# Three raw weight chunks move from SyncE's queue to GpSimd's, each behind a small copy

## The chip, the cores and the metric

One core of a Trainium2 chip runs the whole program. The metric is the device time of one execution in microseconds; the median of three runs counts. The engines are TensorE (PE; its weight loads are PEld), VectorE (DVE), ScalarE (ACT), GpSimd (POOL) and SyncE (SP). SP only issues DMA transfers.

## The reference, cut to what matters

```python
# q, k, v: (4, 8, 576, 64), s: (4, 8, 576)
scores = (1 / sqrt(64)) * q @ k.T
cum = cumsum(maximum(s, 0))
scores = where(causal, -1e9, scores + minimum(-(cum[:, None] - cum[None, :]), 0))
attn = softmax(scores) ; x = attn @ v            # heads side by side: (2304, 512)
h = x @ w_in                                     # moe:  512 -> 2048
x = (h * clip(h + 3, 0, 6) / 6) @ w_out          #       2048 -> 512
h = x @ w2_in                                    # moe2: 512 -> 2048
out = (h * (1 / (1 + exp(-h)))) @ w2_out         #       2048 -> 512
```

The weights are 64-bit numbers; everything else is 32 bits wide.

## The kernel before, in words

**Heads.** Each of the four batches is cut into a part A (256 query rows) and a part B (the other 320). With eight heads this gives 64 heads-with-a-part, here just called heads and numbered from 0 in the order in which they run; A of batch 0 comes first. Head n's tiles have a name, the part, the head's place among eight and a tile number: `pb1A_4_301` is a tile of head 4. A head goes through these steps: SP loads its q, k and v into one tile `in` and then a 4 KB piece of running sums (`inA<-pairs`, from head 4 on `inA<-pair_d`); TensorE makes scores (`ps0`, `ps1`); VectorE masks them and takes the row minimum (L540, `pb0`, `pb1`); ScalarE takes exponentials and their row sums (L558, into one of four tiles `sums`); VectorE adds a small number and takes the reciprocal of the sums (L566, L567); TensorE transposes (`pt`); ScalarE copies the result (`th`); TensorE multiplies by v (`po`); VectorE scales (`xt`). Two such heads are transposed to one piece (`px`, `xA`), which ScalarE and VectorE split into a high and a low half (`xh`, `xl`).

**Slots.** The program is written as slots. In slot k, head k makes its scores, head k-1 (`p1`) its transposes and its product with v. In the first nine slots heads run alone. In that time TensorE also gets three dummy products per head (`keep_clock`, tile `idle`), which read the head's `pb1` tile. From slot 9 on each slot also has a step of the first layer pair: products with `w_in` (`ph`), a gate (`g`, `gh`, `gl`), products with `w_out` (`acc`).

**Weights.** Both layers are cut into 16 chunks each of `w_in` and `w_out`, 512 KB as they lie in memory. They are named i0, o0, i1, o1, ... here (tiles `rawi_0`, `rawo_0`, ...). SP loads a raw chunk (L147); ScalarE makes two passes over it (`fields`, L159 and L160); GpSimd one (L162); VectorE joins the results (L178, L182); ScalarE rounds them to a high half (L120) and VectorE takes the low half (L193). The class `Feed` does this in ticks: at a tick one chunk is asked for, and the one asked for three ticks earlier begins its passes. Three ticks come ahead of slot 0 (i0, o0, i1), 0.4 ticks per slot in slots 0 to 8 (this gives three: o1, i2 and o2), and two per slot after them.

**Order.** The program's text gives priorities; the framework's scheduler fixes at build time in which order each engine's instructions stand, and then each engine works strictly in that order. So an instruction that waits holds up all that stand behind it on its engine. A DMA of SP uses one of eight lanes in turn (DMAHW0 to DMAHW7) and waits until its lane's last transfer has landed.

Of the kernel before, what the change touches and what calls it, by code (L numbers as in the profile page):

```python
# [11 lines left out]
I32 = mybir.dt.int32  # L12
# [15 lines left out]
def kernel(  # L28
# [84 lines left out]
    def pool_copy(o, i):  # L113
        nc.gpsimd.tensor_scalar(  # L114
            out=o, in0=i, scalar1=1.0, scalar2=1.0, op0=ALU.mult, op1=ALU.mult
        )
# [13 lines left out]
    class Chunk:  # L130
# [7 lines left out]
            pool, tag = self.home  # L138
            return pool.tile(shape, dt, tag=tag, name=f"{name}{self.nm}")

        def load(self):
            if self.src.dtype == F32:
                self.val = self.place([P, DM], F32, "raw")
                nc.sync.dma_start(self.val, self.src)
            else:
                raw = self.place([P, 2 * DM], I32, "raw")
                nc.sync.dma_start(raw, self.src.bitcast(I32))  # L147
                words = raw.rearrange("p (n two) -> p n two", two=2)
                self.words = words[:, :, 0], words[:, :, 1]

# [44 lines left out]
    class Feed:  # L195


        def __init__(self, keys, hi_eng, lo_eng):
            self.ch = [Chunk(*k) for k in keys]
            self.hi_eng, self.lo_eng = hi_eng, lo_eng  # L200
            self.t = 0

        def done(self):
            return self.t >= len(self.ch) + 3 + 2

        def tick(self):
            n = len(self.ch)
            t = self.t - 3
            lo = self.lo_eng[t % len(self.lo_eng)] if 0 <= t - 2 < n else ""
            if lo:  # L210
                self.ch[t - 2].high(self.hi_eng[t % len(self.hi_eng)])
            if 0 <= t < n:
                self.ch[t].fields()
            if lo == "p":
                self.ch[t - 2].low(lo)
            if 0 <= t - 1 < n:
                self.ch[t - 1].join()
            if lo == "v":
                self.ch[t - 2].low(lo)
            if self.t < n:  # L220
                self.ch[self.t].load()
            self.t += 1


# [662 lines left out]
    for has_head, has_step in plan:  # L887
        cur = at(k) if has_head else None
        nx = at(k + 1) if has_head else None
        loads = []  # L890
        while has_head and loaded < len(heads) and loaded <= k + (
            2
        ):
            loads.append(heads[loaded])
            loaded += 1
        k += has_head and cur is not None
        tk = [0, 0, 0, 0]
        if not feed.done():
            rate = ((0.4,)*9+(2,))[min(nslot, len(((0.4,)*9+(2,))) - 1)]
            for i in range(4):  # L900
                feed_at += rate / 4
                tk[i] = int(feed_at)
                feed_at -= tk[i]
        slot(cur, p1, p2, nx, loads, has_step, tk)
        if nslot == 9:
            split_rows()
        p1, p2 = cur, p1
        nslot += 1
        if nslot == H + 1:
            p2.av_sum()  # L910
            p2 = None
            split1(0)
            turns["s"] = turns["s"][:1]
        if has_step and step in first_step[1:NB1]:
            blk = first_step.index(step)
            assert k - (cur is not None) >= (blk + 1) * H
            if p2:
                p2.av_sum()
                p2 = None
            if blk == NB1 - 1:  # L920
                cx.close()
                xpool = cx.enter_context(
                    tc.tile_pool(name="xlast", bufs=1, side="right", reuse_waits="tile")
                )
            split1(blk)
            if blk == NB1 - 1:
                break
# [364 lines left out]
```

## Time and profile before

| what | value |
|---|---|
| median of 3 runs | 996.71 us (996.62 to 997.44) |
| profiled execution | 997.93 us, its span 996.1 us |
| PE busy | 973.4 us, 98% of the span |
| DVE busy | 737.3 us, 74% |
| ACT busy | 510.8 us, 51% |
| POOL busy | 266.4 us, 27% |
| mean granted clock of TensorE | 0.992 of full speed |

The span runs from the first to the last instruction of one profiled execution; its own time is 1.8 us longer. Busy shares are averages over stages with different limits, so the tables by stretches say more. The clock is the share of full speed granted to TensorE.

### The profile page before, as it was taken

How to read it: one execution, taken by the hardware profiler on the slowest of the kernel's cores; microseconds unless marked ns; L12 is line 12 of the kernel's file. 1: busy time of each engine (PE TensorE's matmuls, PEld its weight loads, DVE VectorE, ACT ScalarE, POOL GpSimd, SP SyncE). 2: the span in 40 equal slices, each digit the busy share in tenths (PEclk: the TensorE clock that was granted, in tenths of full speed). 3: DMA queues.
4: the chain of work that ended last, by engine and by line, in shares of the span. 5: the costliest groups of instructions: out<-in, count | busy, mean ns of one | idle time of the engine just before them, and what ended most of it. 6: DMA issues, size and time to landing. Idle time of an engine off the chain costs nothing.

```text
span 996.1 us, 17938 instructions
## 1 busy us (share of the span) xinstructions
PE 973.4 (98%) x6268; PEld 896.2 (90%) x6268; DVE 737.3 (74%) x1757; ACT 510.8 (51%) x1177; POOL 266.4 (27%) x323
## 2 busy tenths in 40 slices
PE   8998999999999999999999999999999999999997
PEld 5888999999999999999997877898988989889996
DVE  6899998888789888988866899779674434743343
ACT  6898645555455555555546566455443323432332
POOL 2122433343333443433425466425000000000000
PEclk9899999999999999999999999999999999999999
DMA  5885122312222223222215967434354233442421
GB/s 176 238 285 187 41 55 76 90 49 60 83 77 75 72 59 92 60 61 83 60 32 180 394 225 239 163 116 190 135 193 169 81 141 116 162 154 75 148 75 64
DMA packets 54419, 125.41 MB, mean 126 GB/s; under 512 B 12332, under 2 KB 34076, under 8 KB 51000
## 3 DMA queue, kind: packets, MB, share of 16 engines
q1 hardware_dynamic: 53880, 123.60, 37.7%
q8 instruction: 50, 0.82, 0.3%
q10 hardware_dynamic: 448, 0.66, 0.2%
q14 instruction: 41, 0.34, 0.1%
HBM read 99.52 MB, written 24.69 MB: 125 GB/s over the span
## 4 chain that ended last, share of the span: by engine, by line
PE 74%; DVE 12%; DMA 4%; issue 4%; POOL 3%; ACT 1%; SPq 1%; POOLq 0%; DVEq 0%; ACTq 0%
PE a L1089 6%; PE a L1090 6%; PE a L1091 6%; PE h L1072 5%; PE h L1074 5%; PE h L1073 5%; PE ph L266 5%; PE ph L267 4%; PE ph L268 4%; PE acc L306 4%; PE acc L305 4%; PE acc L307 4%; PE poB L678 3%; DMA rawi<-in_w2i_dram 2%; POOL rawi L167 2%
## 5 line engine op out<-in xcount | busy, mean ns | idle before, releaser
L266 PE MATMUL ph<-xh,wi 128*128 128x256 f32 (+1 forms) x512 | 153.7, 302 | 4.4 <-DVE g L279 4.2
L306 PE MATMUL acc<-gl,wo 128*128 128x256 f32 (+1 forms) x512 | 151.6, 298 | 1.6 <-DVE gl L286 1.6
L267 PE MATMUL ph<-xl,wi 128*128 128x256 f32 (+1 forms) x512 | 151.4, 296 | 0.0
L268 PE MATMUL ph<-xh,wi 128*128 128x256 f32 (+1 forms) x512 | 151.2, 295 | 0.0
L307 PE MATMUL acc<-gh,wo 128*128 128x256 f32 (+1 forms) x512 | 150.3, 295 | 0.0
L305 PE MATMUL acc<-gh,wo 128*128 128x256 f32 (+1 forms) x512 | 143.6, 297 | 0.0
L1131 ACT ACTIVATE gh<-h 128x384 fp32r<-128x384 f32 x96 | 50.3, 524 | 178.7 <-DVE h L1139 178.5
L1089 PE MATMUL a<-wo,gh 128*128 128x512 f32 x288 | 113.6, 395 | 1.5 <-ACT gh L1131 1.1
L1090 PE MATMUL a<-wo,gh 128*128 128x512 f32 x288 | 113.1, 393 | 0.0
L266 PEld LDWEIGHTS ph<-xh,wi 128*128 128x128 f32 x512 | 96.9, 189 | 9.6 <-PE acc L307 1.9
L306 PEld LDWEIGHTS acc<-gl,wo 128*128 128x128 f32 x512 | 96.6, 189 | 5.7 <-DVE gl L286 2.7
L267 PEld LDWEIGHTS ph<-xl,wi 128*128 128x128 f32 x512 | 97.1, 190 | 3.1
L268 PEld LDWEIGHTS ph<-xh,wi 128*128 128x128 f32 x512 | 96.9, 189 | 3.0
L307 PEld LDWEIGHTS acc<-gh,wo 128*128 128x128 f32 x512 | 96.6, 189 | 3.3
L305 PEld LDWEIGHTS acc<-gh,wo 128*128 128x128 f32 x512 | 95.4, 188 | 3.5 <-DVE gh L122 0.2
L1091 PE MATMUL a<-wo,gl 128*128 128x512 f32 x288 | 90.5, 393 | 0.0
L1133 DVE TENSOR_TENSOR gl<-h,gh 128x384 fp32r<-128x384 f32 x96 | 53.4, 556 | 40.4 <-ACT h L1132 38.8
L114 POOL TENSOR_SCALAR gh<-g 128x512 fp32r<-128x512 f32 x68 | 50.0, 738 | 102.7 <-DVE g L279 88.2
L1139 DVE TENSOR_TENSOR h<-h,u 128x384 f32<-128x384 f32 x72 | 40.0, 556 | 49.8 <-PE h L1074 49.4
L1072 PE MATMUL h<-x0t,w 128*128 128x384 f32 x192 | 65.0, 339 | 0.7 <-DVE u L1139 0.7
L1073 PE MATMUL h<-x1t,w 128*128 128x384 f32 x192 | 65.0, 338 | 0.0
L1074 PE MATMUL h<-x0t,w 128*128 128x384 f32 x192 | 64.8, 338 | 0.0
(222 smaller groups left out, 2526.6 us busy)
## 6 DMA issues: line engine op xcount, KB each, us to landing
w<-w_d SPq DMA_DIRECT2D x18, 1792.0 KB
w_d<-w SPq DMA_DIRECT2D x8, 1792.0 KB
k2B<-in_kT_dram SPq DMA_DIRECT2D x64, 144.0 KB
rawi<-in_w1i_dram SPq DMA_DIRECT2D x16, 512.0 KB
rawo<-in_w1o_dram SPq DMA_DIRECT2D x16, 512.0 KB
rawi<-in_w2i_dram SPq DMA_DIRECT2D x16, 512.0 KB
rawo<-in_w2o_dram SPq DMA_DIRECT2D x16, 512.0 KB
q2B<-in_qT_dram SPq DMA_DIRECT2D x64, 80.0 KB
```

The source lines that it names most:

```text
L266: nc.tensor.matmul(o, wih[:, cs], xh[c], start=c == 0, stop=False)
L267: nc.tensor.matmul(o, wih[:, cs], xl[c], start=False, stop=False)
L268: nc.tensor.matmul(o, wil[:, cs], xh[c], start=False, stop=c == NDC - 1)
L305: nc.tensor.matmul(a, woh[:, cs], gh[:, jj, :], start=b0, stop=False)
L306: nc.tensor.matmul(a, woh[:, cs], gl[:, jj, :], start=False, stop=False)
L307: nc.tensor.matmul(a, wol[:, cs], gh[:, jj, :], start=False, stop=b1)
L1072: nc.tensor.matmul(ps, w[:, 0, cs], xh[:, c, :], start=c == 0, stop=False)
L1073: nc.tensor.matmul(ps, w[:, 0, cs], xl[:, c, :], start=False, stop=False)
L1074: nc.tensor.matmul(ps, w[:, 1, cs], xh[:, c, :], start=False, stop=c == 1)
L1089: nc.tensor.matmul(accs[t], gh[:, k, cs], woh, start=b0, stop=False)
L1090: nc.tensor.matmul(accs[t], gh[:, k, cs], wol, start=False, stop=False)
L1091: nc.tensor.matmul(accs[t], gl[:, k, cs], woh, start=False, stop=b1)
```

## The change: what it does

In slots 1 to 8, when there is a head k-1, the feed's chunk is loaded by GpSimd instead of SP. Ahead of the load GpSimd copies two numbers of that head's `sums` into the corner of the raw tile that the load will overwrite. So the load can't start before those sums exist. Three chunks fall into these slots: o1 behind head 1's sums, i2 behind head 4's, o2 behind head 6's.

```diff
-        def load(self):
+        def load(self, behind=None):
+            queue = nc.sync if behind is None else nc.gpsimd
             if self.src.dtype == F32:
                 self.val = self.place([P, DM], F32, "raw")
-                nc.sync.dma_start(self.val, self.src)
+                queue.dma_start(self.val, self.src)
             else:
                 raw = self.place([P, 2 * DM], I32, "raw")
-                nc.sync.dma_start(raw, self.src.bitcast(I32))
+                if behind is not None:
+                    pool_copy(f32(raw[:1, : behind.shape[-1]]), behind)
+                queue.dma_start(raw, self.src.bitcast(I32))
...
             self.t = 0
+            self.behind = None
...
             if self.t < n:
-                self.ch[self.t].load()
+                self.ch[self.t].load(self.behind)
...
                 feed_at -= tk[i]
+        feed.behind = p1.sums[:1, :2] if p1 and nslot <= H else None
         slot(cur, p1, p2, nx, loads, has_step, tk)
```

The scheduler orders several engines anew. The line numbers of the changed kernel are 3 to 5 higher. The first place is SP's queue at head 4's loads. Before, SP has there:

```order
L419 DMA inA_4_251<-in_qT_dram 64x256
L420 DMA inA_4_251<-in_kT_dram 64x256
L409 DMA inA_4_251<-in_v_dram 128x128
L147 DMA rawo_1_261<-in_w1o_dram 128x1024
L429 DMA inA_4_251<-pair_d 2x512
L419 DMA inA_5_294<-in_qT_dram 64x256
```

and in the changed kernel:

```order
L423 DMA inA_4_251<-in_qT_dram 64x256
L424 DMA inA_4_251<-in_kT_dram 64x256
L413 DMA inA_4_251<-in_v_dram 128x128
L433 DMA inA_4_251<-pair_d 2x512
L423 DMA inA_5_295<-in_qT_dram 64x256
```

The chunk o1 is gone from between head 4's v and its row of `pair_d`. On TensorE the scores of head 4 wait for three of these loads (here lanes 5, 6 and 1) and for VectorE; before, with the dummy products of heads 2 and 3 ahead of them, these rows are:

```order
L86 MATMUL idle<-pb1A_2_226,busy 128x256
L86 LDWEIGHTS busy
L86 MATMUL idle<-pb1A_3_265,busy 128x256 [waits Activation_49]
L86 LDWEIGHTS busy
L86 MATMUL idle<-pb1A_3_265,busy 128x256
L86 LDWEIGHTS busy
L86 MATMUL idle<-pb1A_3_265,busy 128x256
L518 MATMUL ps0A_4_310<-inA_4_251 128x128 [waits DMAHW5_49,DMAHW6_49,DMAHW1_49,DVE_49]
```

and in the changed kernel:

```order
L86 MATMUL idle<-pb1A_2_226,busy 128x256
L522 MATMUL ps0A_4_311<-inA_4_251 128x128 [waits DMAHW5_49,DMAHW6_49,DMAHW0_49,DVE_49]
L522 MATMUL ps1A_4_314<-inA_4_251 128x256 [waits DVE_49]
L86 LDWEIGHTS busy
L86 MATMUL idle<-pb1A_3_266,busy 128x256 [waits Activation_49]
```

The scores moved ahead of head 3's dummy products.

The second place is ScalarE at o1's passes. Before:

```order
L120 CAST wi_1_572<-magi_1_450 128x512
L159 ACTIVATE rawo_1_261<-rawo_1_261 128x512
L160 ACTIVATE mago_1_531<-rawo_1_261 128x512
L558 ACTIVATE pb0A_4_301,sums_127<-pb0A_4_301,mxA_4_300 128x128
L558 ACTIVATE pb1A_4_302,sums_127<-pb1A_4_302,mxA_4_300 128x256
L558 ACTIVATE pb0A_5_334,sums_129<-pb0A_5_334,mxA_5_333 128x128
L120 COPY thA_2_289<-pt0A_2_285 128x384
L558 ACTIVATE pb1A_5_335,sums_129<-pb1A_5_335,mxA_5_333 128x256
L731 CAST xh_0_506<-xA_0_282 128x256
L120 COPY thA_3_322<-pt0A_3_318 128x384
```

and in the changed kernel, from head 5's second exponential on:

```order
L562 ACTIVATE pb1A_5_336,sums_129<-pb1A_5_336,mxA_5_334 128x256
L120 COPY thA_2_290<-pt0A_2_286 128x384
L735 CAST xh_0_509<-xA_0_283 128x256
L162 ACTIVATE rawo_1_261<-rawo_1_261 128x512
L163 ACTIVATE mago_1_534<-rawo_1_261 128x512
L120 COPY thA_3_323<-pt0A_3_319 128x384
L562 ACTIVATE pb0A_6_381,sums_131<-pb0A_6_381,mxA_6_380 128x128
L162 ACTIVATE rawi_2_361<-rawi_2_361 128x512
L163 ACTIVATE magi_2_577<-rawi_2_361 128x512
L562 ACTIVATE pb1A_6_382,sums_131<-pb1A_6_382,mxA_6_380 128x256
```

o1's two passes moved from ahead of head 4's exponentials to behind `xh_0`; those of i2 stand between head 6's two exponentials, as before.

The third place is where o2 is asked for and read. GpSimd has in the changed kernel, with what each row waits for (DMASW0 to 2 are the three loads):

```order
L114 TENSOR_SCALAR rawo_1_261<-sums_129 1x2 [waits DVE_49,Activation_49,Pool_49]
L150 DMA rawo_1_261<-in_w1o_dram 128x1024 [waits Pool_49]
L114 TENSOR_SCALAR rawi_2_361<-sums_127 1x2 [waits DVE_49,Activation_49]
L150 DMA rawi_2_361<-in_w1i_dram 128x1024 [waits Pool_49]
L165 TENSOR_SCALAR rawo_1_261<-rawo_1_261 128x512 [waits DMASW0_49,Activation_49]
L165 TENSOR_SCALAR rawi_2_361<-rawi_2_361 128x512 [waits DMASW1_49,Activation_49]
L114 TENSOR_SCALAR rawo_2_459<-sums_131 1x2 [waits DVE_49,Activation_49]
L150 DMA rawo_2_459<-in_w1o_dram 128x1024 [waits Pool_49]
L165 TENSOR_SCALAR rawo_2_459<-rawo_2_459 128x512 [waits DMASW2_49,Activation_49]
```

and ScalarE there:

```order
L562 ACTIVATE pb1A_0_464,sums_127<-pb1A_0_464,mxA_0_462 128x256
L162 ACTIVATE rawo_2_459<-rawo_2_459 128x512
L163 ACTIVATE mago_2_620<-rawo_2_459 128x512
L562 ACTIVATE pb0A_1_496,sums_129<-pb0A_1_496,mxA_1_495 128x128
L562 ACTIVATE pb1A_1_497,sums_129<-pb1A_1_497,mxA_1_495 128x256
L120 COPY thA_6_439<-pt0A_6_435 128x384
L735 CAST xh_2_517<-xA_2_432 128x256
L120 COPY thA_7_484<-pt0A_7_480 128x384
```

where it has before (heads 8 and 9 are called `A_0` and `A_1` again, of the next batch):

```order
L558 ACTIVATE pb1A_0_461,sums_127<-pb1A_0_461,mxA_0_459 128x256
L120 COPY thA_6_437<-pt0A_6_433 128x384
L731 CAST xh_2_514<-xA_2_430 128x256
L159 ACTIVATE rawo_2_457<-rawo_2_457 128x512
L160 ACTIVATE mago_2_617<-rawo_2_457 128x512
L120 COPY thA_7_481<-pt0A_7_477 128x384
L558 ACTIVATE pb0A_1_493,sums_129<-pb0A_1_493,mxA_1_492 128x128
L558 ACTIVATE pb1A_1_494,sums_129<-pb1A_1_494,mxA_1_492 128x256
```

o2's load stands behind GpSimd's pass over i2. On ScalarE, o2's passes moved ahead of `thA_6` and `xh_2`, and head 9's exponentials ahead of these too.

## Rows read from the trace of the kernel before

**Rows 1.** Stretches (us); busy us (instructions) of each engine, granted clock, DMA share, GB/s
```profile
20.00:50.00 30.00, 27.98 (x170) 25.76 (x170) 23.99 (x87) 23.63 (x66) 4.42 (x6) 0.77 0.80 230
50.00:80.00 30.00, 27.79 (x217) 25.93 (x216) 30.00 (x91) 29.18 (x73) 6.83 (x9) 1.00 0.88 285
...
100.00:130.00 30.00, 28.14 (x234) 27.08 (x233) 29.81 (x65) 18.30 (x40) 12.93 (x16) 1.00 0.17 45
130.00:500.00 370.00, 369.16 (x3043) 364.74 (x3042) 320.36 (x909) 196.00 (x523) 141.16 (x209) 1.00 0.25 70
```

The columns after the stretch's length are PE, PEld, DVE, ACT and POOL.

**Rows 2.** Timeline of TensorE at head 4: start, length, line, [idle before <-releaser]
```profile
17.91 0.50 PE L86 MATMUL idle<-pb1A,busy 128*128 128x256 bf16 x3 [0.23 <-ACT pb1A L558]
...
19.79 0.46 PE L518 MATMUL ps0A<-inA 66*128 66x128 f32 x2 [0.23 <-DVE sums L567]
```

**Rows 3.** Timeline of VectorE: head 2's scores, head 1's reciprocal, head 4's sums
```profile
16.66 0.41 DVE L540 CUSTOM_DVE_ANT_0 pb1A<-ps1A,cmask 128x256 f32<-128x256 f32 x1
...
19.03 0.15 DVE L567 RECIPROCAL sums<-sums 128x2 f32<-128x2 f32 x1
...
23.11 0.17 DVE L566 TENSOR_SCALAR sums<-sums 128x2 f32<-128x2 f32 x1
```

**Rows 4.** Timeline of SyncE's queue: the issues of o1 and head 4's row
```profile
16.15 0.43 SPq L147 DMA_DIRECT2D rawo<-in_w1o_dram  x1
16.63 0.29 SPq L429 DMA_DIRECT2D inA<-pair_d  x1
```

**Rows 5.** Timeline of ScalarE from 19 to 36 us
```profile
19.07 0.62 ACT L120 CAST wi<-magi 128x512 fp32r<-128x512 f32 x1
19.81 0.68 ACT L159 ACTIVATE rawo<-rawo 128x512 int32<-128x512 uint32 x1
...
20.95 0.39 ACT L558 ACTIVATE pb0A<-pb0A,mxA 128x128 f32<-128x128 f32 x1
...
25.48 0.39 ACT L731 CAST xh<-xA 128x256 fp32r<-128x256 f32 x1
...
27.78 0.40 ACT L558 ACTIVATE pb0A<-pb0A,mxA 128x128 f32<-128x128 f32 x1 [0.90 <-DVE mxA L540]
...
33.47 0.49 ACT L558 ACTIVATE pb1A<-pb1A,mxA 128x256 f32<-128x256 f32 x1
...
35.06 0.48 ACT L120 COPY thA<-pt0A 128x384 f32<-128x384 f32 x1 [1.00 <-PE pt0A L586]
...
35.74 0.68 ACT L159 ACTIVATE rawo<-rawo 128x512 int32<-128x512 uint32 x1
```

**Rows 6.** Stretches around the two falls of the granted clock (columns as in rows 1)
```profile
17.00:20.00 3.00, 1.88 (x15) 1.27 (x14) 2.86 (x18) 2.68 (x9) 0.00 (x0) 1.00 0.75 236
20.00:29.00 9.00, 8.80 (x44) 7.88 (x43) 6.15 (x25) 6.01 (x18) 0.65 (x1) 0.62 0.56 151
38.00:41.00 3.00, 1.55 (x13) 1.21 (x12) 2.49 (x10) 2.68 (x9) 0.27 (x1) 0.97 0.76 203
```

**Rows 7.** The line that issues raw chunks: duration in ns, min/median/max
```profile
L147 SPq DMA_DIRECT2D rawo<-in_w1o_dram x16: 327/432/1622, 5.3 to 82.4; - x16
```

**Rows 8.** Timeline of the first 10 us: two loads' issues and first readers
```profile
0.73 0.41 SPq L347 DMA_DIRECT2D irow<-in_s_dram  x1
...
2.64 0.59 DVE L348 TENSOR_SCALAR irow<-irow 32x576 f32<-32x576 f32 x1 [1.25 <-DMA irow<-in_s_dram]
...
4.85 0.43 SPq L147 DMA_DIRECT2D rawi<-in_w1i_dram  x1
...
9.21 0.68 ACT L159 ACTIVATE rawi<-rawi 128x512 int32<-128x512 uint32 x1 [3.59 <-DMA rawi<-in_w1i_dram]
```

**Rows 9.** Timeline of GpSimd: its pass over chunks o0 and i1
```profile
11.81 0.65 POOL L162 TENSOR_SCALAR rawo<-rawo 128x512 f32<-128x512 f32 x1 [0.63 <-ACT mago L160]
13.20 0.92 POOL L162 TENSOR_SCALAR rawi<-rawi 128x512 f32<-128x512 f32 x1 [0.74 <-ACT magi L160]
```

**Rows 10.** The DMA view from 15 to 23 us in 40 slices of 0.2 us
```profile
GB/s 0 0 0 159 169 0 87 169 87 108 167 120 287 61 266 287 287 410 461 384 220 144 133 82 228 218 100 141 138 46 159 149 90 213 149 82 205 0 0 123
```

## What the change was expected to do

> **What bounds the kernel now.** I read the table of stretches first, to see which engine is full where. From 130 to 500 us TensorE is busy 369.16 of 370 us, and it stays the bound to the end; there no load can help [rows 1]. Before that the table shows two other stages. From 50 to 80 us VectorE is busy 30.00 of 30, and 29.81 of 30 from 100 to 130. From 20 to 50 us no engine is full all the time: VectorE is busy 23.99 of 30, so 6.0 us idle [rows 1]. That is the most that a smoother opening can give: what VectorE does earlier there it need not do later, and it is the bound until TensorE takes over at 130. All three moved loads lie in this stretch.
>
> Next I read TensorE around the loads, in order of time. The scores of head 4 (tile ps0A) start at 19.79 us, and the trio of dummy products for head 2 ends at 18.41 (17.91 + 0.50) [rows 2]. The view puts the wait on VectorE's reciprocal, but the scores don't read that. The build's list, shown with the change, says what they wait for: three loads of head 4 and a VectorE read of their PSUM bank, which was done long before (head 2's piece, begun at 16.66) [rows 3]. So a load is late. It is the 4 KB row from pair_d, issued at 16.63, right behind the 512 KB chunk o1 issued at 16.15 [rows 4]. ScalarE begins to read o1 at 19.81 [rows 5], 0.02 us after the scores: both land together, the small load behind the big one. I infer this; no view shows a landing by itself.
>
> Third, the granted clock: 1.00 from 17 to 20 us, with TensorE busy 1.88 of 3, then 0.62 on average from 20 to 29 [rows 6]: the lower level, 1.2 GHz instead of 2.4, in 0.38 x 2 x 9 = 6.8 us. The gap before head 4's scores lies just ahead of that fall.
>
> **What the change does, step by step.** o1, i2 and o2 leave SP's queue. Three issues of 0.33 to 1.62 us go [rows 7]; SP is ahead of its readers, so by themselves they are worth nothing, and the cover would be gone only if heads waited for SP's issue.
>
> *Head 4.* Its pair_d load takes o1's place, 16.15. The nearest load with nothing ahead of it is the first one: issued at 0.73, read at 2.64, so 1.91 us [rows 8]. It lands at 18.06, so the scores start behind the trio at 18.41 instead of 19.79: 1.38 us earlier.
>
> *ScalarE, first place.* o1's two passes stand at 19.81 to 20.95, ahead of head 4's exponentials [rows 5]; in the new order they stand behind the copy xh_0. Head 4's exponentials can follow the cast that ends at 19.7, a lead of 1.25. I take this, the smaller of the two.
>
> *Clock.* TensorE at half speed for 6.8 us loses up to 3.4; VectorE's 6.15 busy us of the 9 from 20 to 29 [rows 6] would let most of it be gained. But a gap like the old one opens when the queue waits for o1. I take a third, 1.1, so the lead at xh_0 is 2.35.
>
> *o1.* The small copy waits for head 1's reciprocal, done at 19.18 (19.03 + 0.15) [rows 3]. The copy is 1x2; nothing like it ran on GpSimd, where the nearest operation, on 128x512, takes 0.65 [rows 9]. I take 0.1, with 0.65 as the upper end. Nor did a load go over GpSimd's queue. From SP o1 took 3.66 us from issue to its reader (16.15 to 19.81); the chunk at the start, with two more right behind it, took 4.36 (4.85 + 4.36 = 9.21) [rows 4, 5, 8]. What GpSimd adds is bounded below by a gain of about 0.6 (the rival below) and above by 2.5, SP's longest issue and a pass of GpSimd's in its way (1.62 + 0.92) [rows 7, 9]; I take 0.6, near SP's usual issue (0.43), which is the row most like it. Landing: 19.3 + 3.66 + 0.6 = 23.56. ScalarE comes to it at 25.48 - 2.35 + 0.39 = 23.52: no wait.
>
> *i2.* Held by head 4's sums. Their first half ran at 23.11 [rows 3]; with a lead of 1.25, both parts and the copy (0.16 + 0.15 + 0.1) it is issued at 22.3 and lands at 26.56. ScalarE gets there after o1's passes (1.14), a copy thA (0.48) and an exponential (0.40) [rows 5]: 23.56 + 2.02 = 25.58. It waits 1.0 us, with the exponentials of heads 6 to 8 and the transposes that need them queued behind. It goes on at 26.56 against 28.18 before (27.78 + 0.40): the lead is 1.6.
>
> *o2.* In GpSimd's queue its copy stands behind i2's own pass. So it is issued at 26.56 + 1.14 + 0.65 + 0.1 = 28.45 and, with head loads and the next chunk beside it, lands after 4.36 + 0.6, at 33.4. ScalarE is at that place when head 8's second exponential is done, 33.96 - 1.62 = 32.3, and waits 1.1 us. Its pass starts at 33.4 against 35.74: 2.35 earlier. But thA_6 and xh_2, which stood ahead of it, now stand behind it and head 9's exponentials: 33.4 + 1.14 + 0.40 + 0.49 = 35.4 against 35.06, 0.4 later. Between a lead of 2.35 and a lag of 0.4 the middle is 1.0; I take 1.2, nearer to the lead, since what fills VectorE after 50 us [rows 1] waits for the chunks' passes, and those come early.
>
> *Sum.* -1.2 us, carried by VectorE to 129 us and by TensorE to the end. Against the profiled execution, 997.93 us (span 996.1), that is 996.7; that execution is 1.2 us above the median of the runs, 996.71, so the median should be 995.5. A measurement here tells a change from none beyond about 0.2%, 2.0 us.
>
> **A rule weighed against the rows.** On GpSimd the same pass took 0.65 us at 11.81 and 0.92 at 13.20 [rows 9]: a delay of 0.27. The Trainium skill (SBUF — State Buffer, section "SBUF: two separate sides") says that a load issued from GpSimd has its descriptors written by GpSimd's cores, which are locked out of a shared port while VectorE runs certain copies, so that 620 ns become about 3100. No run here shows it yet. By the rows the delay stays within the 0.6 taken above and the sum is -1.2; by the page's figures it would be an estimated 2.5 us more on each load, and the sum would turn positive.
>
> **Rivals.**
> *The loads come fast (faster, 993.7).* A chunk alone in its queue need not share with heads: the wire showed 384 to 461 GB/s in three slices of o1's passage and at most 287 in any other of the 40 [rows 10]; 512 KB at 430 is 1.2 us, and with the 1.91 of an unhindered load 3.1. Then o1 lands at 22.4, i2 at 25.4, and o2, issued at 27.3, at 30.4 to 31, before ScalarE is there. The lead stays at 2.8 (28.18 - 25.4) and up. With 3.0: 996.71 - 3.0 = 993.7. It needs a clock that doesn't fall at 20 us. Against it: other chunks and heads are on the wire too.
>
> *GpSimd's issue is slow (slower, 999.2).* Each extra microsecond e of latency counts once at i2 and again at o2, since o2 is asked for only after i2's pass. o2's pass starts at 33.4 + 2(e - 0.6), which meets the old 35.74 at e = 1.8; from there the change loses. At e = 2.5, the upper bound above, o2's pass starts at 37.2, 1.5 late, and thA_6 with its transposes and products 4.2 late. In the middle, with part caught up in VectorE's idle time: +2.5. For it: the chain of three, each with a queue behind it. Against it: GpSimd is busy 4.42 of 30 us here [rows 1]. It is also where the page's rule above would lead.
>
> *The clock falls once more (slower, 998.2).* While ScalarE waits for o2 TensorE gets no exponentials. The same kind of gap, 1.55 of 3 us busy from 38 to 41, stands before the second fall [rows 6]. A fall of 6.8 us that TensorE feels in half costs 1.7 to 3.4; less the 1.2: +1.5.
>
> *Nothing happens (996.7).* If the pair_d load was not what head 4 waited for, the order moves and the sum stays. The Trainium skill (DMA: Bandwidth & Descriptors, "Issuing engines are not separate DMA queues") says that loads from several engines share the same sixteen engines and only issue time is saved. Head 4's wait behind o1 speaks for a gain beyond that.
>
> **How the numbers follow.** The forecast (995.5, its own range 994.7 to 996.3) has 0.36, fast loads 0.28, slow issue 0.17, the extra fall 0.09, nothing 0.10. Faster by over 0.2% (below 994.7): fast loads and some of the forecast's edge, 0.33. Slower (above 998.7): most of slow issue and half of the fall, plus what the new order does elsewhere up to 200 us, 0.22. Within: 0.45. The range, 993.0 to 999.0, holds the forecast, both smaller rivals and part of the two larger ones.
>
> **What would show it.** Right: head 4's scores at 18.3 to 18.6; o1, i2 and o2 read near 23.6, 26.6 and 33.4; ScalarE idle about 1 us before i2 and o2; VectorE's idle time from 20 to 50 us down from 6.0 to about 4.8, and all after 130 us shifted by the same. Wrong, if head 4's scores stay at 19.8, if GpSimd's loads need over 6 us, or if the clock is low in another number of stretches than two.

## The result: 12.4 us slower, and the profile after

| | before | after |
|---|---|---|
| median | 996.66 us (995.23 to 997.44, 4 runs) | 1009.07 us (1007.30 to 1011.41, 4 runs) |
| ratio | | 1.0122, 95% interval 1.0086 to 1.0157 |
| profiled execution | 997.93 us, span 996.1 | 1011.41 us, span 1009.6 |
| mean granted clock, profiled execution | 0.992 | 0.983 |
| TensorE at the lower clock, mean of a run | 13 us (30 runs) | 33 us (4 runs) |

The last line is worked out from each run's span and mean granted clock: (1 - clock) x 2 x span, since the lower level is half of full speed. The prediction, 995.5 with a range of 993.0 to 999.0, was wrong in sign.

The changed kernel by stretches, to be held against [rows 1] (columns as there):

```profile
20.00:50.00 30.00, 27.16 (x137) 23.16 (x135) 20.23 (x79) 20.94 (x61) 6.00 (x11) 0.66 0.75 228
50.00:80.00 30.00, 27.16 (x189) 25.34 (x188) 28.66 (x82) 27.09 (x63) 7.11 (x9) 0.88 0.79 265
100.00:130.00 30.00, 27.86 (x217) 26.72 (x217) 29.45 (x69) 19.72 (x46) 9.57 (x13) 0.94 0.17 45
130.00:500.00 370.00, 369.24 (x3045) 364.88 (x3045) 316.50 (x899) 195.37 (x520) 138.88 (x207) 1.00 0.25 70
```

VectorE's idle time from 20 to 50 us is now 9.8 us instead of 6.0. From 130 to 500 us TensorE does as many instructions as before, 3045 to 3043, so most of the time was lost earlier. To see where, count TensorE's instructions in three stretches. Before:

```profile
0.00:20.00 20.00, 16.65 (x76) 8.81 (x77) 12.53 (x40) 12.39 (x31) 6.13 (x20) 1.00 0.56 172
20.00:60.00 40.00, 37.45 (x241) 34.45 (x240) 33.99 (x116) 33.63 (x90) 6.89 (x10) 0.83 0.83 237
60.00:130.00 70.00, 63.39 (x508) 60.17 (x509) 68.35 (x172) 54.98 (x130) 22.74 (x30) 1.00 0.46 149
```

and after:

```profile
0.00:20.00 20.00, 16.59 (x70) 9.38 (x71) 11.80 (x35) 11.14 (x28) 6.15 (x20) 0.91 0.49 149
20.00:60.00 40.00, 37.15 (x190) 32.62 (x189) 29.69 (x105) 30.33 (x82) 8.34 (x15) 0.66 0.72 219
60.00:130.00 70.00, 61.42 (x472) 57.28 (x472) 68.09 (x171) 55.79 (x130) 20.22 (x26) 0.98 0.48 160
```

By 130 us TensorE is 6 + 51 + 36 = 93 instructions behind. At the 8.22 per us of its full stretch (3043 in 370) that is 11.3 us, most of the 13.5 us between the two spans: 6.9 us by 60 us, where the loads moved, and 4.4 us from 60 to 130, where none did. This split is one of counts and not of causes. From 60 to 130 us VectorE, the bound there, does as much as before (68.09 busy us and 171 instructions against 68.35 and 172). And followed by the work itself, most of the loss is there early. The 24th product with `w_in` starts here before:

```profile
48.12 0.28 PE L268 MATMUL ph<-xh,wi 128*128 128x256 f32 x1
```

and here after:

```profile
56.65 0.41 PE L272 MATMUL ph<-xh,wi 128*128 128x256 f32 x1
```

8.5 us later; the 1,500th of them starts 11.2 us later, at 596.47 instead of 585.26. From 20 to 60 us TensorE is as busy as before (37.15 against 37.45) and does a fifth less: the clock is 0.66 instead of 0.83, and 0.17 x 40 = 6.8 us.

The opening, in order of time. First GpSimd's own row, the small copies (L114) and the loads (L150):

```profile
20.10 0.18 POOL L114 TENSOR_SCALAR rawo<-sums 1x2 f32<-1x2 f32 x1 [5.25 <-DVE sums L571]
20.63 0.75 POOL L150 DMA_DIRECT2D rawo<-in_w1o_dram  x1 [0.35 <-POOL rawo L114]
23.02 0.18 POOL L114 TENSOR_SCALAR rawi<-sums 1x2 f32<-1x2 f32 x1 [1.64 <-DVE sums L571]
23.51 0.58 POOL L150 DMA_DIRECT2D rawi<-in_w1i_dram  x1 [0.31 <-POOL rawi L114]
...
32.93 0.58 POOL L150 DMA_DIRECT2D rawo<-in_w1o_dram  x1 [0.30 <-POOL rawo L114]
```

ScalarE at the three chunks, o1, i2 and o2 (L162 is their first pass):

```profile
26.44 0.65 ACT L162 ACTIVATE rawo<-rawo 128x512 int32<-128x512 uint32 x1 [1.75 <-DMA rawo<-in_w1o_dram]
...
29.01 0.71 ACT L162 ACTIVATE rawi<-rawi 128x512 int32<-128x512 uint32 x1 [0.60 <-DMA rawi<-in_w1i_dram]
...
39.69 0.67 ACT L162 ACTIVATE rawo<-rawo 128x512 int32<-128x512 uint32 x1 [3.60 <-DMA rawo<-in_w1o_dram]
```

From issue to reader they take 5.8, 5.5 and 6.8 us, and ScalarE waits for each. What that does to TensorE, which needs the copies thA behind these passes:

```profile
25.56 0.60 PE L522 MATMUL ps1A<-inA 66*128 66x256 f32 x2
28.07 0.88 PE L697 MATMUL poA<-inA,thA 128*128 128x64 f32 x6 [1.91 <-ACT thA L120]
```

and the clock around it, by stretches (columns as in [rows 1]):

```profile
20.00:29.00 9.00, 6.90 (x52) 5.62 (x51) 5.47 (x26) 5.63 (x18) 2.33 (x5) 1.00 0.71 197
26.30:29.70 3.40, 1.63 (x12) 1.53 (x13) 1.61 (x5) 2.65 (x7) 0.64 (x1) 1.00 0.68 203
29.70:57.00 27.30, 26.54 (x111) 23.46 (x110) 20.52 (x69) 21.11 (x57) 5.68 (x9) 0.50 0.78 244
```

Before, the clock fell at 20 us [rows 6]; now it holds from 20 to 29. But from 26.3 to 29.7 TensorE is busy 1.63 of 3.4 us, and right behind that the clock stands at the lower level for 27.3 us in one piece, though TensorE's row is busy 26.54 of them. In the kernel before it was low for 6.8 us twice.

### The profile page after: what moved, and what is told of

Read it like the earlier page. It is cut to its first block, busy times and chain, and to the rows that moved or that the text cites. A ratio compares the mean times of both kernels' runs of the same rounds, so it can differ in the third digit from the quotient of the medians.

```text
span 1009.6 us, 17968 instructions
## 1 busy us (share of the span) xinstructions
PE 982.6 (97%) x6268; PEld 903.1 (89%) x6268; DVE 737.5 (73%) x1757; ACT 511.4 (51%) x1177; POOL 269.6 (27%) x329
## 3 DMA queue, kind: packets, MB, share of 16 engines
q0 software_dynamic: 432, 1.57, 0.5%
## 4 chain that ended last, share of the span: by engine, by line
PE 74%; DVE 10%; issue 5%; DMA 5%; POOL 3%; ACT 2%; SPq 1%; POOLq 0%; DVEq 0%; ACTq 0%
PE a L1094 6%; PE a L1095 6%; PE a L1096 6%; PE ph L270 5%; PE h L1077 5%; PE ph L271 5%; PE h L1079 5%; PE h L1078 5%; PE ph L272 5%; PE acc L310 4%; PE acc L311 4%; PE acc L309 4%; PE poB L682 3%; DMA rawi<-in_w2i_dram 2%; POOL rawi L170 2%
## 5 line engine op out<-in xcount | busy, mean ns | idle before, releaser
L1136 ACT ACTIVATE gh<-h 128x384 fp32r<-128x384 f32 x96 | 50.3, 524 | 178.0 <-DVE h L1144 177.9
L270 PEld LDWEIGHTS ph<-xh,wi 128*128 128x128 f32 x512 | 98.0, 191 | 7.6 <-DVE g L283 1.8
L272 PEld LDWEIGHTS ph<-xh,wi 128*128 128x128 f32 x512 | 98.4, 192 | 3.0
L114 POOL TENSOR_SCALAR gh<-g 128x512 fp32r<-128x512 f32 x68 | 48.2, 710 | 96.2 <-DVE g L283 89.0
```

What stands on the lines that cost most here:

```text
L270: nc.tensor.matmul(o, wih[:, cs], xh[c], start=c == 0, stop=False)
L272: nc.tensor.matmul(o, wil[:, cs], xh[c], start=False, stop=c == NDC - 1)
```

## Experiments

Eighteen runs; after_again is the changed kernel once more. "Low" is TensorE's time at the lower clock, mean of a kernel's runs, worked out as above; the last two columns count TensorE's instructions in the profiled execution. The counts hold the dummy products: before_keep4 has 8 more than the kernel before, before_keep6 and after_keep6 24, before_keep_on and after_keep_on 9, before_keep_on1 3, and before_keep0 has 24 fewer. One execution can lie off the median: only_o1's took 998.72 us, hold_on_sp's 1001.37, before_keep_on's 995.02, p2_on_act's 1006.05 and after_keep_on's 1009.50. The difference is to the kernel before on the same chips.

| kernel | median us | difference | low us | 0 to 60 us | 60 to 130 us |
|---|---|---|---|---|---|
| before | 996.7 to 997.9 | | 13 | 317 | 508 |
| after | 1009.07 | +12.4 | 33 | 260 | 472 |
| after_again | 1008.71 | +11.1 | 34 | 253 | 490 |
| only_o1 | 1001.38 | +3.5 | 17 | 321 | 506 |
| only_i2 | 1005.18 | +7.3 | 24 | 293 | 477 |
| only_o2 | 1003.00 | +5.1 | 17 | 312 | 509 |
| hold_on_sp | 1003.60 | +6.0 | 19 | 323 | 482 |
| hold_on_act | 1004.17 | +6.6 | 15 | 325 | 489 |
| hold_p2 | 1006.55 | +9.0 | 33 | 259 | 516 |
| p2_on_act | 1009.00 | +11.4 | 37 | 232 | 513 |
| no_hold | 1009.11 | +11.8 | 34 | 231 | 503 |
| copies_only | 1001.40 | +4.0 | 9 | 315 | 507 |
| one_copy | 1002.19 | +4.6 | 11 | 311 | 506 |
| before_keep4 | 1005.38 | +8.0 | 19 | 324 | 507 |
| before_keep6 | 1000.28 | +2.9 | 14 | 314 | 486 |
| before_keep_on | 998.38 | +0.8 | 7 | 339 | 519 |
| before_keep_on1 | 1001.94 | +4.3 | 17 | 318 | 500 |
| after_keep_on | 1005.70 | +7.8 | 22 | 269 | 492 |
| after_keep6 | 1010.40 | +13.3 | 33 | 296 | 486 |
| before_keep0 | 1006.82 | +9.7 | 45 | 211 | 504 |

**One chunk at a time.** The feed's line, with (1, 2, 3), (4, 5) or (6, 7, 8):

```diff
-        feed.behind = p1.sums[:1, :2] if p1 and nslot <= H else None
+        feed.behind = p1.sums[:1, :2] if p1 and nslot in (1, 2, 3) else None
```

> Only o1 comes over GpSimd's queue behind head 1's sums; i2 and o2 stay in SP's queue. Clock theory: the changed kernel lost its 12 us because TensorE ran dry ahead of 29.7 us and the clock then stayed at 1.2 GHz for 27 us instead of twice 7; if o1's late landing is what ran it dry, the low stretch is over 20 us again and the time 1005 or more; if it is not, the low stretches sum to under 17 us and the time is 996 to 999. Waits theory: each late chunk costs just what ScalarE waits for it, 1.75 us here, 998.5. Order theory: the scheduler's new order costs by itself; the time is over 1002 with low stretches of under 17 us in sum.

> Only i2 comes over GpSimd's queue behind head 4's sums. Clock theory: i2 was the smaller wait (0.60 us); without o1's wait the gap ahead of 29.7 us closes, the low stretches sum to under 17 us and the time is 996 to 999. Waits theory: i2 now is reached earlier, so 1 to 2 us of wait, 998. Order theory: over 1002 with low stretches of under 17 us in sum.

> Only o2 comes over GpSimd's queue behind head 6's sums. Clock theory: o2's wait (3.60 us in the changed kernel) fell into a stretch that was at the low clock already, so it did not start the long one; alone it either makes one short fall more, 998 to 1001, or starts a long one, over 1005. Waits theory: 1000.3. Order theory: over 1002 with low stretches of under 17 us in sum.

All three are slower than the waits theory says, by 2.7 to 7.2 us. The low stretches of the profiled executions sum to 10.2, 17.1 and 6.8 us up to 130 us, so no long one appeared. The order theory's condition was met by o2 (1003.00 us); i2 has 0.1 us too much of low clock for it and o1, 1001.38, not quite the time. The three differences add up to 15.9 us, more than all three chunks together cost, so they aren't the prices of three loads.

only_o1 says most. ScalarE stands there in the order of the changed kernel up to o2's passes (xh_0, o1, thA_3, i2, ...), but for thA_4, which changed places with an exponential, and it waits for o1:

```profile
24.64 0.66 ACT L162 ACTIVATE rawo<-rawo 128x512 int32<-128x512 uint32 x1 [1.45 <-DMA rawo<-in_w1o_dram]
...
26.51 0.67 ACT L162 ACTIVATE rawi<-rawi 128x512 int32<-128x512 uint32 x1
```

Yet its opening is whole: 241 instructions from 20 to 60 us, as before. So o1 behind GpSimd's queue and a wait of 1.45 us for it needn't lose the opening. In the changed kernel i2 is late as well, directly behind, and then o2, ahead of thA_6.

A single load in GpSimd's queue is little slower than one in another (in hold_on_sp o1 took 4.33 us to its reader): the trace's DMA view gives for o1 alone, from issue to landing in the last column,

```profile
rawo<-in_w1o_dram POOLq DMA_DIRECT2D x1, 512.0 KB, 4.7
```

and 4.7 and 4.2 for the others, where all three together took (x2 is o1 and o2)

```profile
rawo<-in_w1o_dram POOLq DMA_DIRECT2D x2, 512.0 KB, 6.2
...
rawi<-in_w1i_dram POOLq DMA_DIRECT2D x1, 512.0 KB, 5.4
```

**The same loads in another queue.** The copies stay, the queue is SP's or ScalarE's:

```diff
-            queue = nc.sync if behind is None else nc.gpsimd
+            queue = nc.sync                                     # hold_on_sp
+            queue = nc.sync if behind is None else nc.scalar    # hold_on_act
```

> The changed kernel with the three loads back in SP's queue, still behind the small copies; what GpSimd's queue itself adds is gone, what the hold adds stays, and SP's later loads now wait behind it. GpSimd's-queue theory (the chunks land late because that queue needs 5.4 to 6.7 us where SP's took 3.6 to 4.5): o1 and i2 land 1 to 2 us earlier, TensorE's gap ahead of 29.7 us closes, the time is 997 to 1001. Hold theory (they are asked for too late for the place that the order gives them): the gap stays, a low stretch over 15 us, 1004 to 1012. Order theory (the new order costs 4 to 7 us of TensorE's idle time wherever the chunks come from): 1001 to 1004 with no low stretch over 10 us.

> The changed kernel with the three loads in ScalarE's queue, behind the same small copies: no SP load waits behind them and no software queue carries them, but ScalarE pays an issue for each. GpSimd's-queue theory: loads of 3.6 to 4.5 us, the time is 997 to 1001. Hold theory: still late, a low stretch over 15 us, 1004 to 1012. Order theory: 1001 to 1004 with no low stretch over 10 us.

Half of the loss goes. The order theory came nearest, 1001 to 1004 with no low stretch over 10 us; each has one of 10.2. The order did move too: thA_6 stands ahead of head 9's exponentials again, i2's passes behind both of head 6's, and in hold_on_act thA_3 ahead of o1's. So queue and order aren't separated here. In hold_on_act ScalarE hardly waits for the chunks:

```profile
23.57 0.67 ACT L162 ACTIVATE rawo<-rawo 128x512 int32<-128x512 uint32 x1 [0.22 <-DMA rawo<-in_w1o_dram]
...
33.51 0.67 ACT L162 ACTIVATE rawo<-rawo 128x512 int32<-128x512 uint32 x1 [0.42 <-DMA rawo<-in_w1o_dram]
```

Its stretches:

```profile
20.00:60.00 40.00, 36.51 (x242) 32.58 (x241) 32.42 (x112) 33.86 (x90) 6.72 (x11) 0.87 0.78 244
60.00:130.00 70.00, 62.04 (x489) 57.26 (x488) 68.54 (x182) 55.17 (x134) 28.25 (x31) 1.00 0.50 155
130.00:500.00 370.00, 366.91 (x3025) 362.58 (x3024) 316.88 (x893) 196.09 (x521) 141.86 (x208) 1.00 0.25 69
```

So the opening is whole again (242 instructions against 241 before), and yet the kernel is 6.6 us slower: 19 instructions are missing from 60 to 130 us and 18 behind that. None of the three moved loads is late by more than 0.42 us. From 60 to 130 us ScalarE waits 3.0 us for later chunks, against 1.8 before, and the order on the engines is another. Which of the two costs the 6.6 us isn't shown.

**The same loads, asked for earlier.** Each copy waits for one head earlier, over GpSimd's queue (hold_p2) or ScalarE's (p2_on_act):

```diff
-        feed.behind = p1.sums[:1, :2] if p1 and nslot <= H else None
+        feed.behind = p2.sums[:1, :2] if p2 and nslot <= H else None
```

> The changed kernel with each copy behind the sums of one head earlier (0, 3 and 5 instead of 1, 4 and 6), so each load is asked for some 2 to 3 us earlier over the same queue. ScalarE's order is the same through o1's and i2's passes; o2's pass stands earlier. Hold theory: o1 and i2 land ahead of ScalarE, TensorE's gap ahead of 29.7 us closes, the time is 997 to 1002. GpSimd's-queue theory: the loads still need 5.4 to 6.7 us; with the earlier ask o1's wait of 1.75 us is gone all the same, so this run does not tell these two apart; 997 to 1002. Order theory: 1001 to 1006 without waits at o1 and i2.

> The same earlier copies as in hold_p2 (1006.55 us), but the loads ride ScalarE's queue. GpSimd's-queue theory: each load lands 1 to 2.5 us sooner, low clock falls from some 33 us a run to under 20, and the time is 1000 to 1004. Order theory alone (the queue is innocent, orders differ by luck): 1005 to 1008.

Both went against the theories. In hold_p2 o1 was issued at 19.39 us instead of 20.63, read at 25.23, and ScalarE still waited 2.41 us for it; the three loads were in flight together and took 5.8 to 7.0 us. And in p2_on_act, without GpSimd's queue, the time is no better, 1009.0. There ScalarE waits for i2

```profile
26.03 0.68 ACT L162 ACTIVATE rawi<-rawi 128x512 int32<-128x512 uint32 x1 [1.53 <-DMA rawi<-in_w1i_dram]
```

and TensorE has, busy only 31.95 of 40 us and at a clock of 0.68,

```profile
20.00:60.00 40.00, 31.95 (x150) 25.91 (x150) 30.45 (x100) 31.46 (x82) 8.11 (x13) 0.68 0.82 257
```

So GpSimd's queue isn't needed for such a loss. It isn't free either: issued within 0.2 us of each other in these two kernels, i2 and o2 took 6.56 and 7.36 us to their readers in hold_p2 and 5.48 and 5.41 in p2_on_act. What these two share with the changed kernel, its second run, after_keep_on and after_keep6 is ScalarE's order: o2's passes and later heads' exponentials stand ahead of thA_6 (in these two ahead of thA_4 as well), so transposes and products of heads that are done wait behind work that is not. In the four with a whole opening and a chunk moved or held (only_o1, only_o2, hold_on_sp, hold_on_act) thA_6 stands ahead of head 9's. That order alone doesn't bring the whole loss: before_keep6, below, has o2's passes and head 9's exponentials ahead of thA_6 too, with no load moved, and is 2.9 us slower.

**Without the hold.** The copies are left out, the loads stay in GpSimd's queue and are issued at 3.4 to 4.7 us:

```diff
-                if behind is not None:
-                    pool_copy(f32(raw[:1, : behind.shape[-1]]), behind)
```

> The three loads in GpSimd's queue without the small copies: all three are asked for at the start, beside i0, o0 and i1. They share the wire with the first loads (1.5 MB more, at 300 to 460 GB/s 3 to 5 us of wire), so ScalarE's first pass, at 9.21 us before, comes 1 to 4 us later, but o1, i2 and o2 lie there long before they are read. GpSimd's-queue theory (the loss is their late landing): no wait and no long low stretch at 30 us; the start's delay is partly made up; 998 to 1002. Order theory: the same and 4 to 7 us for the order, 1002 to 1006. Clock theory: if the start's delay makes TensorE run dry ahead of 20 us, a low stretch there instead; 1000 to 1006.

1009.11 us, beyond every theory's range: the first chunk i0 is read at 12.18 us instead of 9.21, TensorE's first 20 us hold 45 instructions instead of 76, and the clock is low from 16.2 to 36.7 and again from 50.3 to 64.0. It says that six chunks at once starve the start; on o1 to o2 it says nothing.

**Controls: no load moved.** copies_only makes the three copies into a spare tile and leaves the loads in SP's queue; one_copy makes one such copy in slot 2 of the kernel before. The spare tile (`aside`, 8 bytes in each partition) is in these two, and in no other kernel. before_keep4, before_keep6, before_keep_on and before_keep_on1 give TensorE a few more dummy products.

```diff
+    aside = cpool.tile([P, 2], F32, tag="aside", name="aside")   # one_copy, copies_only
...
+        if nslot == 2:                                        # one_copy
+            pool_copy(aside[:1, :2], p1.sums[:1, :2])
...
-            keep_clock(3, heads_of(p1.prob[1]))
+            keep_clock(4, heads_of(p1.prob[1]))               # before_keep4; 6 in before_keep6
...
-        if p1 and not mm:
+        if p1 and (not mm or step < 3):                       # before_keep_on; 1 in before_keep_on1
```

> A control for the order: the three loads stay in SP's queue where they were; only the three small copies are made, into a tile that nothing reads. No load is held, no engine that matters has more to do (3 x 0.2 to 0.5 us on GpSimd, which is idle there); the scheduler orders the engines anew from there on. Order theory (part of the loss, some 6 us with the loads in ScalarE's or SP's queue, is the price of another order than the one before, in the stretch from 60 to 200 us): 1000 to 1004. Hold theory (those 6 us come from loads asked for later): 995 to 999.

> A third control: the kernel before plus a single 1x2 copy on GpSimd from head 1's sums into a tile that nothing reads, 0.2 us on an idle engine. Order theory: it moves the scheduler to another order and costs 2 us or more, 999 to 1005. If the order costs nothing: 996 to 998.5, as the kernel before.

> A second control: the kernel before with four dummy products per head instead of three, no load moved. The eight more (half a group of 0.5 us each three, so 0.17 each) are at most 1.3 us of TensorE work in a stretch in which TensorE is not the bound. Order theory: another order, 999 to 1004 unless it keeps the clock up. Hold theory and GpSimd's-queue theory: no change, 995 to 999.

> The kernel before with six dummy products per head. At most 24 x 0.17 = 4 us more of TensorE work ahead of 45 us. Clock theory: the low stretches (13.6 us before) shrink, worth up to 6.8 us, 993 to 998. Order theory: 999 to 1004. GpSimd's-queue and hold theory: no load moves, 995 to 1000.

> A control: the kernel before with the nine dummy products in slots 9 to 11, no load moved. They are at most 4.5 us of TensorE work at full speed if nothing hides them; the scheduler orders the engines anew. Clock theory: the fall at 40.84 us (6.8 us at half speed, worth 3.4) may go; 994 to 999. Order theory: any new order costs some us, 1000 to 1004, with no more low clock than before.

> The kernel before with three more dummy products, in slot 9 alone. Clock theory: less low clock than before (13 us a run) and, if the order is no worse, 994 to 997, a gain. Order theory: 999 to 1004 whatever the clock does.

one_copy is 4.6 us slower (ratio 1.0048, interval 1.0024 to 1.0071) and copies_only 4.0, with no more low clock a run than before. Both expectations took it that the order would move. It didn't: in both traces TensorE, VectorE, ScalarE and GpSimd have the instructions of the kernel before, by name and shape, in the same order (buffer numbers left out, and but for the copies), and so have the DMA issues. The loss builds up behind 130 us, where TensorE is full:

```profile
130.00:500.00 370.00, 369.73 (x3012) 366.36 (x3013) 316.94 (x904) 195.66 (x523) 140.39 (x207) 1.00 0.25 70
```

```profile
130.00:500.00 370.00, 370.00 (x3020) 366.88 (x3019) 317.35 (x902) 196.08 (x523) 141.39 (x209) 1.00 0.25 70
```

The first is one_copy, the second copies_only: 31 and 23 instructions fewer than before. The products themselves follow each other more slowly. Here are one product with `w_in` and the fifteenth behind it, before:

```profile
299.70 0.28 PE L266 MATMUL ph<-xh,wi 128*128 128x256 f32 x1
...
301.40 0.28 PE L266 MATMUL ph<-xh,wi 128*128 128x256 f32 x1
```

and in one_copy:

```profile
302.58 0.28 PE L267 MATMUL ph<-xh,wi 128*128 128x256 f32 x1
...
304.36 0.28 PE L267 MATMUL ph<-xh,wi 128*128 128x256 f32 x1
```

That is 113 ns from start to start and 119. Over all such pairs from 200 to 500 us the median is 118 ns in one_copy and copies_only, and 114 in each of the other eighteen traces, whatever their order. Behind 130 us this makes up the 4.8 and 4.7 us that the two traces lose there. So these two controls don't test the order. They show a price of 4 to 5 us that goes with the spare tile, and not with the copies, which the changed kernel makes too. The tile is allotted ahead of others; that it shifts what TensorE reads is argued, not shown, since no view gives addresses.

The other four do have another order. They are 0.8 to 8.0 us slower, before_keep_on being level with the kernel before (ratio 1.0004, 0.9982 to 1.0025); but they hold up to 4 us of dummy products more, and a low clock of 7 to 19 us. before_keep4 loses most, behind 130 us: 2,994 instructions up to 500 us instead of 3,043, TensorE idle 3.8 us there instead of 0.8. So another order can cost some us, and no run here prices it by itself. The idea that a kept clock would beat the kernel before found no support: before_keep_on has half the low clock and the same time.

**The clock as a cause.** after_keep_on adds dummy products in slots 9 to 11 of the changed kernel, after_keep6 has six per head, before_keep0 takes the heads' dummy products out of the kernel before.

```diff
-        if p1 and not mm:                                     # before_keep0
-            keep_clock(3, heads_of(p1.prob[1]))
```

> The changed kernel with the three dummy products per head also in the first three slots that have a step (slots 9 to 11), where it has none. They add about 9 x 0.5 us of TensorE work at most, 4.5 us, if nothing else changes. Clock theory: the low clock lasts because TensorE's work from 30 to 57 us does not lift it; with dummy products in it the long stretch ends earlier (under 20 us) and the time falls below 1006. Waits theory and order theory: the time is 1009 to 1014, no better, since neither waits nor the order are mended.

> The changed kernel with six dummy products per head instead of three (24 more, at most 4 us of TensorE work in the opening). Loads, copies and queue stay. Clock theory: low clock falls from 33 us a run to under 20, the order's 4 us stay, and the time is 1000 to 1005. Work theory (late chunks leave the engines without work, the clock only follows): 1007 to 1011 even with less low clock.

> The kernel before without the dummy products of the heads (27 fewer); no load moves, no chunk is late. Clock theory: low clock rises from 13 us a run to over 30, and the time with it, by 4 to 6 us and the order's share of about 4: 1003 to 1008. Work theory: the time is the order's alone, 998 to 1002, whatever the clock.

> The changed kernel unaltered, for a second profile and more times. Clock theory: again a low stretch of over 20 us from about 27 to 30 us on, ScalarE waiting 1.5 us or more for o1, 1007 to 1010. If the long low stretch does not come again while the time stays over 1006, the clock is not what costs.

before_keep0 has its chunks where the kernel before has them (ScalarE waits for one chunk from 19 to 45 us, for 0.59 us), and the clock is at the lower level all the way:

```profile
20.00:60.00 40.00, 37.36 (x148) 32.72 (x148) 33.38 (x108) 33.35 (x84) 7.92 (x11) 0.50 0.82 257
```

With 24 dummy products fewer it still does 317 - 211 - 24 = 82 other instructions less by 60 us, and takes 1006.82 us, as the clock theory said. after_keep_on gave back 3.4 us with 11 us less low clock a run; in its profiled execution, the slowest of its four, the clock was still low for 23.9 us in one piece, over the 20 that the clock theory allowed. after_keep6 decided nothing: its dummy products didn't keep the clock (33 us low, as without them), so the time stayed as well. after_again repeats the time, ScalarE's waits (1.48, 1.16 and 4.57 us) and the 33 us of low clock a run, though in its profiled execution the clock was low for 3.4 and 17.1 us between 20 and 60, and not over 20 us in one piece as expected. Its counts split the loss another way than the first execution's, 64 instructions by 60 us and 18 behind, at the same order on all engines.

## Why the prediction was wrong

**What bounds the kernel, and head 4's scores: right.** With pair_d no longer behind o1, the scores of head 4 start behind head 2's trio. In hold_on_act this is plain (predicted 18.3 to 18.6, before 19.79 [rows 2]):

```profile
17.56 0.50 PE L86 MATMUL idle<-pb1A,busy 128*128 128x256 bf16 x3 [0.23 <-ACT pb1A L562]
17.90 0.38 PE L522 MATMUL ps0A<-inA 66*128 66x128 f32 x2
```

In the profiled execution of the changed kernel they came at 20.16, likewise behind the trio (19.82): there the clock was low from 16.0 to 19.5 us, before any chunk was held. The lead exists, and the clock does hold from 20 to 29 us. Neither outweighs what stands against it. The other signs of being wrong that the prediction named came: a load of over 6 us, and three low stretches up to 130 us instead of two.

**The load over GpSimd's queue: the mis-sized term.** "What GpSimd adds" was taken as 0.6 us, of bounds -0.6 to 2.5. From issue to reader it measured 26.44 - 20.63 = 5.81, 5.50 and 6.76 us, where the sum had 4.26, 4.26 and 4.95: so 2.2, 1.8 and 2.4 us were added, not 0.6. That is the deciding point of the slow-issue rival, 1.8, or past it. ScalarE waited 1.75, 0.60 and 3.60 us where 0, 1.0 and 1.1 were forecast, and thA_6 came at 41.69 instead of 35.4. The rival had this mechanism, but its reason, a slow issue, isn't what the rows show: the issues are 0.75 and 0.58 us long. The lateness comes behind the issue. The Trainium skill (SBUF — State Buffer, "SBUF: two separate sides") gives figures by which a load of GpSimd comes an estimated 2.5 us later; this run's 1.8 to 2.4 are near that, but single loads in the same queue landed 4.2 to 4.7 us after their issue, so the trace doesn't show it as a price of the queue as such. With three loads close together, i2 and o2 took 1.1 and 2.0 us longer in it than in ScalarE's queue (hold_p2 against p2_on_act).

**The clock: the step that failed.** It was costed at a gain of 1.1 us, and a further fall, the rival, at a loss of 1.7 to 3.4. Both took a fall to last 6.8 us. A gap opened in TensorE's work from 26.3 to 29.7 us behind o1's and i2's late passes, as the rival said of a wait for o2, but the fall behind it lasted 27.3 us, and TensorE, not VectorE, was full in it (VectorE 20.52 of 27.30). A fall isn't a fixed price: at half speed TensorE was the fuller engine of the opening, so the length of the fall counts. The late chunks aren't needed for the fall itself. In hold_on_act, where ScalarE hardly waits for them, it comes at the same place, behind a gap too, but lasts 10 us:

```profile
23.00:26.70 3.70, 2.68 (x21) 2.34 (x21) 2.37 (x10) 3.05 (x9) 0.67 (x1) 1.00 0.71 212
26.70:37.00 10.30, 10.24 (x44) 9.13 (x43) 6.21 (x22) 6.63 (x19) 1.46 (x3) 0.50 0.49 156
```

Over the 237 runs whose clock is listed a straight line (each kernel with a constant of its own) gives 0.23 us of span for each us at the lower clock, with 1.4 us left over; the 20 us more that the changed kernel has are then an estimated 4.7 us. before_keep0 shows that a low clock of this length can go with a loss of this size without a late chunk; its order is new too, so its 9.7 us aren't the clock's alone. (The rival's own sum was off by little: the middle of 1.7 to 3.4 less 1.2 is 1.35, not 1.5.)

**The order: priced at one place, and there by the wrong landing.** The sum took the new order on the engines, up to 200 us, at nothing but its effect at three places, and put what it does elsewhere into the tail of the chances. In the opening the forecast saw thA_6 behind o2's passes and head 9's exponentials and priced that at 0.4 us, by a landing that came 6 us later than taken. What the order costs elsewhere isn't shown: the controls that keep the loads where they were either kept the order as well, or changed dummy work and clock with it. hold_on_sp and hold_on_act, which lose 26 and 19 instructions from 60 to 130 us with the opening whole, speak for some price.

**The sum as measured.** By 130 us TensorE is 11.3 us behind, and 8.5 of them are there at the 24th product with `w_in`: late chunks, the clock that fell among them, and the order of ScalarE. Behind 500 us come 2 us more, where TensorE is busy 483.96 of 490 us instead of 485.86; why isn't shown. Together that is 13.3 of the 13.5 us between the spans.

**What stays open.** How the opening's loss divides between late chunks, ScalarE's order and the clock can't be told: the three went together in all five kernels that lost it by holding loads, and no kernel had all three chunks late at full clock. Nor is it shown why the clock stayed low for 27 us with TensorE's row full, or why a spare tile slows products that never read it. None of the kernels beats the one before.

## What to carry to other kernels

A control that is meant to move the order alone has to be laid beside the kernel before, instruction by instruction: here two of them kept the order and lost 4.0 and 4.6 us by slower products, more than the edit was forecast to be worth. A slowdown of that size from one spare tile has to be ruled out before an order, a queue or a clock is blamed. A load that is held back until just before its reader needs it has its worst landing, not its usual one, as the price, since its transfers meet all others of the same microseconds. And a gap on an engine whose clock can fall is to be priced by how long the clock may stay down, at the rate of whichever engine is the bound at that clock.

## What the runs showed of the hardware

The same three loads, 432 packets and 1.57 MB, took from 19 to 41 us a larger share of the 16 DMA engines' time in GpSimd's queue (changed kernel, first row; columns: packets, MB, share) than in ScalarE's (hold_on_act, second fence):

```profile
q0 software_dynamic: 432, 1.57, 24.8%
```

```profile
q10 hardware_dynamic: 432, 1.57, 19.6%
```

That is 0.248 x 22 x 16 / 432 = 202 ns of engine time a packet against 160. In the pair hold_p2 and p2_on_act, from 15 to 41 us, it was 19.5 against 18.6%, so the surplus isn't constant. A 1x2 copy on GpSimd took 0.18 us twice and 0.48 once, and the load behind it was issued 0.30 to 0.35 us after the copy's end. With a spare tile of 8 bytes a partition in the program, TensorE's products of 256 columns, in the same order and at a granted clock of 1.00, started 118 ns apart (median from 200 to 500 us) instead of 114. And runs of one and the same kernel differ in low clock: 30 runs of the kernel before had mean clocks of 0.987 to 0.998 and times of 994.7 to 1004.3 us, so one profile of a kernel like this isn't its clock.
